# Loading w2 in blocks of six from ScalarE's DMA queue, with a new cost model and new priorities for the order of all instructions

## The chip, the cores and the metric

The kernel runs on one core of one Trainium2 chip. The metric is the device time of one execution in microseconds (us). A single core has no second die to compare with, so all runs count as fast ones, but executions of one program still differ: most by under 0.5%, a few by 1%. Medians over several executions are given with their range.

## The reference, cut to what matters

Two layers, each made of sliding-window attention and an MLP, on 2048 tokens of width 576:

```python
# x: [1, 2048, 576]; 32 heads of 18, window 256; MLP width F = 4608; bf16 inputs
x = x + A(layernorm(x))       # qkv = x @ wqkv; masked softmax(q k^T * 18**-0.5) v; @ wo
x = x + B(layernorm(x))       # gelu(x @ w1 + b1) @ w2 + b2
x = x + A(layernorm(x))       # the same weights again
x = x + B(layernorm(x))
```

## The kernel before

The 2048 tokens are worked off in groups of 512, four per layer. Its buffers hold four ninths of w1 and half of w2, so both are loaded anew for each group. Every operation is described once as a task (engine, buffers read and written, an estimated cost, a priority). A scheduler written in Python plays the tasks through on estimated costs and fixes one order of instructions for each engine. `nudge` shifts the priority of whole stages: `q1.0` is a part of the projections of group 1, `t0` the tail of group 0 (output projection, residual, layernorm), `ma0` the first MLP matmuls, and so on.

```python
PL.nudge = {"ld0+": 36.49, "eb0": 11.82, "q1.0": -3.43, ...}        # cut

def w1_load(prio, reads=()):                                        # cut
    dma("sp", w1_sb[:, sl, 0:2048]..., B_w1[0:512, cols]..., cls="w1", cost=0.55, ...)
    for b in range(2):                                              # the last 64 rows
        dma("sp", w1_sb[64 * b:64 * b + 64, sl, 2048:2304]..., cls="w1", cost=0.6, ...)

def w2_load(hf, prio, gate=False):
    for pr in range(NFH // 2):                                      # nine pairs a half
        f0 = hf * NFH + 2 * pr
        dma("sp", w2_sb[:, 2 * pr:2 * pr + 2, :], B_w2[f0 * P:(f0 + 2) * P, :]...,
            writes=[f"w2s{pr}"], cls="w2", ring=9, cost=0.55, lat=2.0, move=0.88, desc=256, prio=prio)

def tail(k, prio):                                                  # cut
    for i in range(nt):                                             # attention output, transposed by DMA
        add("sp", lambda e, i=i: e.dma_start_transpose(attT[:, :, i * 128:(i + 1) * 128], attq[:, i, :]), ...)
    for i in range(nt):
        bs = two_out(lambda c, i=i: attT[...], lambda c, s: wo_sb[...], ...)   # output projection on TensorE

# ln_norm_T, cut: the normalise on VectorE, then a DMA transpose from SyncE
add("dve", lambda e: e.tensor_scalar(xn[:, sl, 0:D], s[:, t, :], mv_all[:, t, 0:1], rstd[:, t:t + 1], ...), cost=0.6, ...)
add("sp", lambda e: e.dma_start_transpose(dst[:, :, i * 128:(i + 1) * 128], xn[:, sl, :]), ...)

def x_load(a, cnt, reads, prio):                                    # the residual, from GpSimd
    dma("pool", x_res[:, a:a + cnt, :], x_dram[...]..., cls="xr", ...)
```

Each DMA is issued by one engine (`"sp"` is SyncE, `"act"` ScalarE, `"pool"` GpSimd), and each engine takes its instructions in the order that the scheduler fixed. Nearly all weights and all transposes go through SyncE.

The softmax here doesn't subtract the row's maximum and nothing guards it: scores larger than these inputs give would overflow.

## Time and profile before

| | before |
|---|---|
| time, median of 3 | 945.84 us (945.45 to 946.3) |
| TensorE busy | 910.2 us of a span of 940.9 us |
| ScalarE busy | 593.4 us |
| bytes in SyncE's queue (q1) | 120.96 MB of 130.10 MB |

TensorE is at work for 97% of the span. What can be won is its idle time and what its records hide, so the waits of TensorE are the view to read, and the other engines matter where they end such a wait. The profiled execution of the kernel before took 942.78 us, some 3 us less than its median. In line numbers, L524 before and L530 after is the helper that issues every plain DMA, so loads are told apart by their tiles and sizes. Three terms recur: a transfer is *issued* while its engine hands it to the DMA engines, and it *lands* when all its data have arrived; the *granted clock* (PEclk) is the share of its full clock that TensorE was given, in these records either 1.00 or, for some us at a time, 0.50 ("half clock").

### The profile page before, as it was taken

Reading aid. Unit: us, or ns where it says so; the run is one execution under the profiler, and the core shown is the slowest. Engines: PE = TensorE matmul, PEld = TensorE weight load, DVE = VectorE, ACT = ScalarE, POOL = GpSimd, SP = SyncE. Lnnn points to the kernel's source line nnn. Section 1 sums busy time; section 2 is a strip of 40 time slices with the busy share of each in tenths; the row PEclk is TensorE's granted clock in tenths of the full one; section 3 lists DMA queues with packets and bytes.
Section 4 is the critical chain, followed back from the end, with each engine's and each line's share of the span. In section 5 each row is a group of like instructions: output and inputs, shape, how many; then the busy total and the mean of one; then the engine's idle time right before and its main releaser. Section 6 shows DMA issues by size and latency. Waiting matters only on the chain. (4 is left out here: it accounts for less than half of the span.)

```text
span 940.9 us, 22724 instructions
## 1 busy us (share of the span) xinstructions
PE 910.2 (97%) x9394; PEld 559.5 (59%) x9394; DVE 319.3 (34%) x796; ACT 593.4 (63%) x717; POOL 372.1 (40%) x507
## 2 busy tenths in 40 slices
PE   9888998999999999989999999999999999999998
PEld 6555474664755747455674666656566574656556
DVE  6647132641217511154420832135132330241001
ACT  3787675576756658656465567756776587852541
POOL 3877352353514425144250644515443163720100
PEclk9999999999999999999999999999999999999999
DMA  9995729725196160965439434594526916094440
GB/s 225 153 219 113 212 60 247 191 56 169 21 218 163 16 204 13 249 130 140 133 45 270 79 93 123 99 252 77 158 71 121 252 52 203 13 233 140 151 140 26
DMA packets 232470, 130.10 MB, mean 138 GB/s; under 512 B 142384, under 2 KB 230192, under 8 KB 232368
## 3 DMA queue, kind: packets, MB, share of 16 engines
q1 hardware_dynamic: 223056, 120.96, 53.8%
q0 software_dynamic: 6880, 5.03, 3.7%
q10 hardware_dynamic: 2432, 2.65, 0.9%
q8 instruction: 75, 1.23, 0.5%
q14 instruction: 27, 0.22, 0.1%
HBM read 91.87 MB, written 2.36 MB: 100 GB/s over the span
## 5 line engine op out<-in xcount | busy, mean ns | idle before, releaser
L744 ACT ACTIVATE pT<-ps 128x1024 bf16<-128x1024 f32 (+2 forms) x384 | 348.3, 970 | 138.7 <-PE ps L735 137.6
L765 POOL TENSOR_SCALAR_AFFINE_SELECT pT<-pT 128x512 bf16<-128x512 bf16 (+1 forms) x368 | 281.8, 789 | 288.9 <-ACT pT L744 258.8
L903 PE MATMUL ps<-w_sb,hT 128*128 128x288 bf16 x2304 | 318.0, 287 | 3.1 <-DVE x_res L816 1.8
L878 ACT ACTIVATE hT<-ps,b1col 128x512 bf16<-128x512 f32 x288 | 197.0, 688 | 176.1 <-PE ps L875 175.9
L875 PE MATMUL ps<-xnTm,w_sb 128*128 128x512 bf16 x1152 | 263.8, 380 | 0.0
L903 PEld LDWEIGHTS ps<-w_sb,hT 128*128 128x128 bf16 x2304 | 212.0, 98 | 74.8 <-issue 15.1
L875 PEld LDWEIGHTS ps<-xnTm,w_sb 128*128 128x128 bf16 x1152 | 106.2, 98 | 142.0 <-issue 26.6
L816 DVE TENSOR_TENSOR x_res<-ps,x_res 128x288 f32<-128x288 f32 x160 | 71.2, 449 | 312.0 <-PE ps L903 242.9
L665 PE MATMUL ps<-wqkv,xnTa 128*128 128x288 bf16 x960 | 136.9, 288 | 6.3 <-DVE qn L700 4.1
L665 PEld LDWEIGHTS ps<-wqkv,xnTa 128*128 128x128 bf16 x960 | 86.4, 98 | 42.5 <-DVE qn L700 8.6
L782 PEld LDWEIGHTS ps<-vA,pT 128*128 128x128 bf16 x2880 | 94.8, 96 | 25.3 <-issue 9.7
L782 PE MATMUL ps<-vA,pT 128*128 128x20 bf16 x2880 | 100.4, 171 | 3.5 <-POOL pT L765 2.7
L700 DVE CAST qn<-ps 128x288 bf16<-128x288 f32 x120 | 54.3, 455 | 106.1 <-PE ps L665 103.5
L885 POOL TENSOR_TENSOR x_res<-x_res,b2bc 128x576 f32<-128x576 f32 x32 | 44.9, 1402 | 97.1 <-ACT hT L878 97.1
L735 PE MATMUL ps<-qT,kT 32*128 32x384 bf16 (+2 forms) x1216 | 64.4, 277 | 3.4 <-DMA kT<-qn 1.2
L591 POOL TENSOR_SCALAR vtmp<-mv_all 128x1 f32<-128x1 f32 (+1 forms) x43 | 8.8, 205 | 116.9 <-DVE mv_all L582 115.7
L665 PE MATMUL ps<-wo_sb,attT 128*128 128x288 bf16 x320 | 45.5, 289 | 6.7 <-DMA attT<-attq 5.8
L580 DVE BATCH_NORM_STATS2 st_all<-x_res 128x6 f32<-128x288 f32 x104 | 44.8, 447 | 7.5 <-DMA x_res<-in_A_x_dram 6.3
L863 PE MATMUL ps<-xnTm,w_sb 64*128 64x512 bf16 x288 | 45.3, 384 | 1.0 <-ACT pT L744 0.7
L603 DVE TENSOR_SCALAR xn<-x_res,mv_all,rstd 128x576 bf16<-128x576 f32 x52 | 38.9, 754 | 15.2 <-DMA xnTm<-xn 5.8
L665 PEld LDWEIGHTS ps<-wo_sb,attT 128*128 128x128 bf16 x320 | 29.6, 98 | 19.9 <-DMA attT<-attq 6.7
L819 DVE TENSOR_TENSOR xn<-ps,x_res 128x288 bf16<-128x288 f32 x32 | 14.4, 454 | 77.2 <-PE ps L903 75.6
(39 smaller groups left out, 270.3 us busy)
## 6 DMA issues: line engine op xcount, KB each, us to landing
w_sb<-in_B_w_dram SPq DMA_DIRECT2D x144, 288.0 KB, 4.5
w_sb<-in_B_w_dram SPq DMA_DIRECT2D x72, 512.0 KB, 4.5
w_sb<-in_B_w_dram SPq DMA_DIRECT2D x144, 32.0 KB, 4.1
x_res<-in_A_x_dram POOLq DMA_DIRECT2D x4, 1152.0 KB, 7.8
out_dram<-xn SPq DMA_DIRECT2D x16, 144.0 KB, 1.8
wqkv<-in_A_wqkv_dram ACTq DMA_DIRECT2D x3, 576.0 KB, 7.2
hT<-in_A_x_dram SPq DMA_DIRECT2D x2, 576.0 KB, 4.4
wo_sb<-in_A_wo_dram ACTq DMA_DIRECT2D x1, 576.0 KB, 6.6
```

The lines of the kernel that those rows point to most:

```text
L665: ins = e.matmul(bank(bs[o])[:, 0:HB], lhs(c), rhs(c, o * HB), start=(c == 0), stop=(c == KD - 1))
L700: add("dve", lambda e, b=bs[o], dst=dst: e.tensor_copy(dst, bank(b)[:, 0:HB].rearrange("p (h d) -> p h d", d=DH)), reads=[bs[o]], writes=[ ...
L735: ins = e.matmul(two(bs[j // 2])[:, j % 2, col:col + nq * 128], k_of(T0 + so)[0][32 * j:32 * j + 32, g, :], qs[32 * j:32 * j + 32, g, qo * ...
L744: add("act", lambda e, h2=h2: e.activation(pT[:, sl, 2 * h2:2 * h2 + 2, lo:hi], two(bs[h2])[:, :, lo:hi], ACT.Exp, scale=SCALE), reads=[bs ...
L765: add("pool", lambda e, ap=ap, pat=pat, sgn=sgn, kind=kind: e.affine_select(ap, ap, pattern=pat, compare_op=(ALU.is_ge if kind == "d" else ...
L782: ins = e.matmul(bank(B_O)[:, o:o + VW], pT[:, sl, j, col + qi * 128:col + (qi + 1) * 128], vA[:, (T0 + so) % VS, 4 * g + j, :], start=(fi ...
L816: add("dve", lambda e: e.tensor_tensor(x_res[:, t, sl], bank(b)[:, 0:HB], x_res[:, t, sl], ALU.add), reads=[b], writes=[f"x{t}h{hh}"], cos ...
L863: ins = e.matmul(bank(bk)[:, 0:n], w1_sb[64 * b:64 * b + 64, sl, col:col + 128], xnTm[64 * b:64 * b + 64, k % 2, 4, 0:n], start=True, stop ...
L875: ins = e.matmul(bank(bk)[:, 0:n], w1_sb[:, sl, col:col + 128], xnTm[:, k % 2, c, 0:n], start=False, stop=(c == 3))
L878: add("act", lambda e, ff=ff, fl=fl, bk=bk: e.activation(hT[:, fl, 0:n], bank(bk)[:, 0:n], ACT.Gelu_apprx_tanh, bias=b1col[:, ff:ff + 1]), ...
L885: add("pool", lambda e, t=t: e.tensor_tensor(x_res[:, t, :], x_res[:, t, :], b2bc[:, :], ALU.add), reads=["b2", f"h{fs[0]}"], writes=X(t), ...
L903: ins = e.matmul(bank(b)[:, 0:HB], hT[:, fl, i * 128:(i + 1) * 128], w2_sb[:, fl, hh * HB:(hh + 1) * HB], start=(fl == 0), stop=(fl == NFH ...
```

## The change

It has three parts. w2 is loaded in blocks of six slices (864 KB) by ScalarE's DMA queue, instead of pairs (288 KB) by SyncE's. The scheduler's model now has a queue for each issuing engine that shares the DMA engines, and operation costs taken from traces. The priorities were found anew by annealing on that model, so every engine's order changes.

```diff
+    WB = 6
-    PL.nudge = {"ld0+": 36.49, "eb0": 11.82, "q1.0": -3.43, ...}
+    PL.nudge = {"le0+": 6.85, "q1.0": -1.09, "q1.1": -1.98, ...}          # all values new; cut
     def w2_load(hf, prio, gate=False):
-        for pr in range(NFH // 2):
-            f0 = hf * NFH + 2 * pr
-            dma("sp", w2_sb[:, 2 * pr:2 * pr + 2, :], ..., writes=[f"w2s{pr}"], cls="w2", ring=9, cost=0.55, ..., desc=256)
+        for b in range(NFH // WB):
+            f0 = hf * NFH + WB * b
+            dma("act", w2_sb[:, WB * b:WB * b + WB, :], ..., writes=[f"w2s{b}"], cls="w2", ring=NFH // WB, cost=0.55, ..., desc=128 * WB)
     # scheduler: one modelled queue for each issuing engine
-                done = max(dma_free, st + t.cost + t.lat) + t.move
+                at = max(served.get(t.eng, 0.0), st + t.cost + min(t.lat, 2.0))
+                done = at + t.move
+                for o in served:
+                    if o != t.eng and served[o] > at:
+                        both = min(t.move, served[o] - at)
+                        served[o] += both
+                        done += both                                     # cut
     # costs, some of about twenty
-            reads=res + [f"mv{t}", f"rstd{t}"], writes=[f"xn{sl}"], cost=0.6, prio=prio)
+            reads=res + [f"mv{t}", f"rstd{t}"], writes=[f"xn{sl}"], cost=0.67 if src is None else 0.45, lat=0.14, prio=prio)
-            reads=[f"vt{t}" for t in ts] + ["nhalf"], writes=rds, cost=0.4, prio=prio)
+            reads=[f"vt{t}" for t in ts] + ["nhalf"], writes=rds, cost=0.4 + 0.155 * n, lat=0.08, prio=prio)
```

## The prediction

> **What bounds the kernel now.** I read the page's busy table first, then the busy time per stretch, the waits of PE, the waits of the DMA queue on SyncE, and last the timeline around the longest waits. The busy table and the slices say TensorE:
>
> ```profile
> PE 910.2 (97%) x9394; PEld 559.5 (59%) x9394; DVE 319.3 (34%) x796; ACT 593.4 (63%) x717; POOL 372.1 (40%) x507
> ...
> PE   9888998999999999989999999999999999999998
> ...
> DMA  9995729725196160965439434594526916094440
> ```
>
> PE stands still for only 940.9 - 910.2 = 30.7 us by these records, and DMA engines, ScalarE and GpSimd all have room. So no change that leaves the matmuls alone can gain more than those 30.7 us plus waits that the records hide. They do hide some: the record of a 128x288 matmul is 287 ns (groups table), yet by their start times such matmuls follow each other every 122 ns, so a wait of 150 ns between two of them does not show as idle.
>
> I therefore also added up the start-to-start distances of all matmuls. At the usual spacing of each kind (122 ns for 288 columns, 216 ns for 512, 25 ns for the 20-column ones) all matmuls but the scores make about 807 us. The score groups and the changes from one kind of matmul to another, at what such a change usually takes here (96 to 260 ns), make about 100 us more. What lies above the usual value is 33 us: 13 us before 94 us, 3.9 us in 141 to 188, 4.5 us in 376 to 423, and mostly 0 to 2 us in other stretches of 47 us. Those 33 us are the whole prize for a better order and better timed transfers, with a few us of ramp, warm-up matmuls and tail beside them.
>
> The stretches show where it stands still (PE busy is the second number, then PEld, DVE, ACT and POOL; near the end PEclk and the DMA share):
>
> ```profile
> 20.00:40.00 20.00, 16.14 (x191) 9.27 (x189) 13.60 (x43) 13.23 (x19) 13.82 (x19) 0.91 1.63 138
> 60.00:80.00 20.00, 17.06 (x277) 11.11 (x277) 9.47 (x25) 17.31 (x21) 14.00 (x20) 1.00 0.80 156
> 160.00:180.00 20.00, 18.04 (x112) 9.99 (x113) 13.26 (x39) 7.17 (x10) 3.41 (x8) 0.91 0.94 247
> 400.00:420.00 20.00, 16.29 (x208) 11.73 (x207) 10.12 (x26) 11.62 (x15) 7.90 (x13) 1.00 0.67 137
> 580.00:600.00 20.00, 20.00 (x303) 14.35 (x300) 4.11 (x10) 16.07 (x18) 12.42 (x17) 1.00 0.01 2
> ```
>
> The ramp (the first 100 us, where w2 plays no part) loses most: 100 - 88.6 = 11.4 us idle. Then two spots stand out. In both, the waits of PE name one cause, the DMA transpose of the attention output:
>
> ```profile
> PE ps L665 <- DMA attT<-attq: 5.8, 2, 3.1
> PE ps L665 <- DVE qn L700: 4.1, 9, 0.9
> PE ps L782 <- POOL pT L765: 2.7, 8, 0.6
> PE ps L735 <- DMA kT<-qn: 2.1, 2, 1.2
> ```
>
> The timeline of the first spot shows SyncE's queue issuing one transpose, then six weight loads in 7.44 us, then the next transpose, while PE waits 3.08 us:
>
> ```profile
> 153.19 1.23 SPq L826 DMA_TRANSPOSE attT<-attq  x1
> ...
> 154.52 7.44 SPq L524 DMA_DIRECT2D w_sb<-in_B_w_dram  x6
> ...
> 161.96 2.00 PE L665 MATMUL ps<-wo_sb,attT 128*128 128x288 bf16 x10 [3.08 <-DMA attT<-attq]
> 162.01 1.29 SPq L826 DMA_TRANSPOSE attT<-attq  x1
> ```
>
> And the queue's own waits show that loads which wait for a buffer hold up everything behind them:
>
> ```profile
> SPq L524 <- PE ps L903: 89.5, 17, 25.8
> ```
>
> These are w2 loads waiting for the second MLP matmuls to free their buffer, up to 25.8 us at a time. Most of it costs nothing, as nothing urgent stood behind.
>
> **What the Trainium skill says.** "DMA: Bandwidth & Descriptors", section "Issuing engines are not separate DMA queues": transfers started from different engines run on the same 16 DMA engines, and a second issuer only saves issue time. The same page, section "Queues, rings and completion order": each DMA engine takes turns between the queues that have work, a packet at a time. So no bandwidth is gained, but a transpose need not stand behind a burst of w2 in the same queue. Before, nearly all goes through one queue (q1, 120.96 MB of 130.10 MB), so the trace can't show it yet. "Trace Analysis", section "Per-instruction lifecycle": the record of such an issue covers descriptor generation, not the movement. The trace agrees: a weight load issues in 0.515 us at the median and lands after 4.5 us. "TensorE: Matmul & The Clock Gate", section "Why this matters for your kernels": idle gaps of about 3 us drop the clock. The trace agrees in part: PEclk is 0.91 in 160 to 180, after the 3.08 us gap, and also in 20 to 40, but stays 1.00 after the 2.68 us gap near 410.
>
> **The change, part by part.**
> *Removed from SyncE:* 144 w2 loads of 288 KB at 0.515 us = 74 us of issuing, more where the ring was full (the longest took 2.834 us). The queue's issuing now is 360 x about 0.55 us for weights (197 us summed from the trace) plus 156 transposes (214 us), so it falls from some 411 us to some 330 us, and the buffer waits leave it as well. Off PE's path except at the two attT spots. There I expect most of the 5.8 us back, some 4.5 us, and the half clock from 173.1 to 176.5 us in the trace, worth 3.4 / 2 = 1.7 us: **-6 us**.
> *Added to ScalarE:* 16 half loads x 3 blocks = 48 issues of 864 KB. Before, ACT issued six loads in 3.76 us, 0.63 us each: 48 x 0.63 = 30 us. The diff's own bookkeeping counts 768 descriptors a block against 2048, so the third block of a half should wait for space, which I guess at 1.5 us: 16 x 1.5 = 24 us more. ScalarE stands still 940.9 - 593.4 = 347 us, so 54 us fit, but it runs in order: an issue ahead of an exp or a gelu delays it. In the busiest mixed stretches (17.3 of 20 us) this can reach PE. I allow **+2 us**.
> *Bytes:* the same, 2.65 MB per half. A block of six is what one matmul task reads anyway, so waiting for six in place of three pairs costs nothing.
> *Moved:* every order on every engine, from new costs and nudges. The new costs agree better with the profile where I can compare: a residual add 0.375 + 0.14 = 0.515 us against a record of 0.449; a normalise 0.67 + 0.14 against 0.754; the small 64-column normalise 0.38 + 0.14 against 0.468, formerly 0.12; rstd for four now 1.02 against about 1.03 in the timeline, formerly 0.4. An order made with such costs should leave fewer of the short waits (qn, affine select, rstd). Of the 33 us above the usual, 6 are counted already; of the other 27 I take a third: **-9 us**. This is a guess, since the ramp's dependencies are real and the old order had been tuned too.
> Sum: -6 + 2 - 9 = -13 us, and I add -1 us for fewer warm-up matmuls filling gaps (62 now, 35 of them before any data is there). 945.84 - 14 = about **932 us**.
>
> **The rivals.**
> *ScalarE becomes the hindrance:* its queue now waits for the second MLP matmuls to free w2, as SyncE did for 89.5 us, and every exp and gelu behind waits too. For it: ScalarE is strictly in order and feeds PE twice, through exp and gelu. Against it: the new order puts issues where the model sees the buffer free, and the engine has 37% room. It would take back 5 to 15 us: 937 to 947.
> *The transfers were hidden anyway:* attT alone is 5.8 us, and most long queue waits have nothing urgent behind them. Then the order alone decides and the gain is under 6 us: 940 to 946.
> *The order is the main thing:* if the corrected model removes most of the 33 us, including the ramp, it saves 20 to 25 us: 921 to 926. Against it: the waits over the usual are near zero already in half of the stretches, and 13 us sit in a ramp whose first steps depend on each other.
>
> **Range and chances.** My sum gives 932; 33 us of prize, none of it needing new resources, makes slower unlikely. A 2% gain needs 926.9 us, thus 19 us, more than half of the prize: 0.27. Within 2%: 0.70. Slower by 2% would need ScalarE to stall for 19 us on PE's path: 0.03. Eight times in ten: 920 to 944.
>
> **What would show it.** Right: PE busy time nearly the same or a little less, idle down from 30.7 to under 20 us; no wait on attT over 1 us; queue waits on w2 gone from SyncE; a second hardware queue with 42 MB (48 x 864 KB); PEclk 1.00 in the stretches after 100 us; 48 issues on ScalarE of 0.6 us at the median with some over 2 us. The step on ScalarE is wrong if its waits on PE within w2 issues add up to over 10 us with PE idle beside them. The step on the order is wrong if idle outside the attT spots stays at some 25 us. The prediction as a whole fails if hardware lets w2 bursts slow the transposes by sharing the engines, so that kT, qT or attT land later than now (3.7 to 4.0 us) and PE waits there in new places, or if the new order cuts the number of changes between kinds of matmul, which I left as it is.

## The result, and the profile after

| | before | after |
|---|---|---|
| median, same rounds | 945.68 us (945.45 to 946.3, 4 runs) | 937.97 us (937.35 to 938.3, 4 runs) |
| ratio | | 0.9917, 95% interval 0.99 to 0.9934: the same within 2% |
| span of the profiled execution | 940.9 us | 936.2 us |

Ratios are the mean time of one kernel's fast runs over that of the other's fast runs of the same rounds, so not quite the ratio of the medians. The gain is 7.7 us where 14 were predicted.

The page of the kernel after, its busy table, TensorE's slices and the two hardware queues (packets, MB, share of the engines' time):

```profile
PE 903.7 (97%) x9336; PEld 562.5 (60%) x9382; DVE 316.5 (34%) x796; ACT 593.9 (63%) x717; POOL 370.5 (40%) x507
...
PE   8798999999999999999999999999999999999998
...
q1 hardware_dynamic: 183888, 78.48, 40.0%
q10 hardware_dynamic: 40064, 45.13, 15.4%
```

The second queue now carries w2, 48 x 864 KB = 42.5 MB more than its former 2.65 MB. The weight loads (PEld) count 12 fewer, which are warm-up matmuls. Matmul records: 9336 against 9382 weight loads, so 46 are missing, and the busy sums of the two traces cannot be subtracted to a few us.

The stretches that the prediction showed, and three more (40 to 60, 820 to 840 of both kernels). Columns: stretch, length, then busy us of PE, PEld, DVE, ACT and POOL with counts, granted clock, DMA share, GB/s. After:

```profile
20.00:40.00 20.00, 16.29 (x198) 10.79 (x199) 14.01 (x42) 11.14 (x16) 12.06 (x16) 0.94 1.78 145
40.00:60.00 20.00, 16.01 (x208) 9.94 (x206) 11.71 (x22) 12.82 (x18) 12.04 (x17) 0.81 1.11 213
60.00:80.00 20.00, 17.59 (x298) 11.11 (x290) 8.44 (x21) 18.91 (x25) 15.12 (x21) 1.00 0.81 148
160.00:180.00 20.00, 19.78 (x133) 10.53 (x132) 8.24 (x25) 11.65 (x16) 2.95 (x6) 1.00 1.16 295
400.00:420.00 20.00, 19.34 (x228) 14.14 (x227) 18.97 (x49) 10.52 (x14) 10.74 (x18) 1.00 0.56 117
...
820.00:840.00 20.00, 18.00 (x109) 9.01 (x108) 10.76 (x30) 9.07 (x14) 2.96 (x8) 1.00 0.86 189
```

And before, for the two stretches that the prediction did not show:

```profile
40.00:60.00 20.00, 18.44 (x286) 11.88 (x285) 10.13 (x24) 16.26 (x23) 15.35 (x22) 1.00 1.24 249
820.00:840.00 20.00, 20.00 (x180) 11.02 (x178) 7.31 (x21) 12.35 (x17) 6.10 (x10) 1.00 0.89 229
```

Both bad spots are mended: TensorE is busy 19.78 us in 160 to 180 where it was 18.04, and 19.34 in 400 to 420 where it was 16.29. But two stretches got worse. In 40 to 60 it fell from 18.44 to 16.01 us of 20, at a mean clock of 0.81 instead of 1.00, and in 820 to 840 from 20.00 to 18.00.

TensorE's waits after (total us, times, longest):

```profile
PE ps L742 <- ACT pT L751: 5.5, 15, 1.1
PE ps L672 <- DVE qn L707: 4.5, 6, 2.0
PE ps L789 <- DVE attq L804: 2.6, 3, 1.4
PE ps L672 <- DMA attT<-attq: 2.1, 2, 1.9
PE ps L672 <- DVE vA L694: 2.0, 4, 1.1
```

The wait on attT fell from 5.8 to 2.1 us. The largest wait is now the one on ScalarE's exponentials, 5.5 us against 1.6 before.

To see where the time went I subtracted from the time, for both traces, the usual cost of every matmul issued so far (by its kind, from the spacing of weight loads). The difference of the two curves, after minus before, is +3.5 us at 160, +0.4 at 180, -2.0 at 400, -5.1 at 420, -7.5 at 800, -4.3 at 860 and -4.8 at 920. (A second working of the same sum gave +3.5, +0.6, -2.0, -5.0, -6.8, -4.9 and -4.8, so single stretches are good to some 0.7 us.) So the ramp lost 3.5 us; the two attT spots gained 3.1 us each; all else between 180 and 800 gained 4.8 us; the stretch of 800 to 860 gave 3.2 us back, and after it some 0.5 us came in again. The sum is the difference of the two spans, 4.7 us; the other 3 us of the median are the lucky execution that was profiled of the kernel before.

The curve leaves out the changes from one kind of matmul to another, and the new order has fewer of them: 762 in place of 788, or 751 in place of 765 without the warm-up matmuls. At the median spacing of each kind of change in the two traces that is about 3 us less, an estimate; no run isolates it.

### The profile page after: what moved, and what is told of

The parts are those of the page before. It is cut to its first block, busy times and chain, and to the rows that moved or that the text cites. A ratio compares the mean times of both kernels' runs of the same rounds, so it can differ in the third digit from the quotient of the medians.

```text
span 936.2 us, 22505 instructions
## 1 busy us (share of the span) xinstructions
PE 903.7 (97%) x9336; PEld 562.5 (60%) x9382; DVE 316.5 (34%) x796; ACT 593.9 (63%) x717; POOL 370.5 (40%) x507
## 4 chain that ended last, share of the span: by engine, by line
PE 82%; DMA 5%; DVE 4%; issue 3%; ACT 2%; POOL 2%; SPq 1%; POOLq 0%; DVEq 0%
PE ps L910 28%; PE ps L882 24%; PE ps L672 13%; PE ps L789 7%; PE ps L742 5%; PE ps L870 4%; DMA attT<-attq 2%; ACT pT L751 2%; DMA hT<-in_A_x_dram 1%; DMA qT<-qn 1%; DVE xn L609 1%; POOL pT L772 1%; PE ps L573 1%; SPq L714 1%; POOL x_res L892 0%
## 5 line engine op out<-in xcount | busy, mean ns | idle before, releaser
L910 PE MATMUL ps<-w_sb,hT 128*128 128x288 bf16 x2304 | 314.0, 286 | 0.4 <-DVE x_res L823 0.4
L882 PE MATMUL ps<-xnTm,w_sb 128*128 128x512 bf16 x1106 | 258.9, 379 | 4.0 <-issue 1.9
L799 DVE RECIPROCAL rinv<-ps 128x16 f32<-128x16 f32 x64 | 16.4, 256 | 72.4 <-PE ps L789 72.4
L742 PEld LDWEIGHTS ps<-qT,kT 32*128 32x128 bf16 x1216 | 19.6, 92 | 33.5 <-issue 22.0
```

The lines of the kernel that those rows point to most:

```text
L742: ins = e.matmul(two(bs[j // 2])[:, j % 2, col:col + nq * 128], k_of(T0 + so)[0][32 * j:32 * j + 32, g, :], qs[32 * j:32 * j + 32, g, qo * ...
L882: ins = e.matmul(bank(bk)[:, 0:n], w1_sb[:, sl, col:col + 128], xnTm[:, k % 2, c, 0:n], start=False, stop=(c == 3))
L910: ins = e.matmul(bank(b)[:, 0:HB], hT[:, fl, i * 128:(i + 1) * 128], w2_sb[:, fl, hh * HB:(hh + 1) * HB], start=(fl == 0), stop=(fl == NFH ...
```

## The experiments

Twelve kernels ran, in three sets of four, each set on another chip with its own runs of the kernel before (medians 946.24, 945.02 and 946.39 us). Medians of different sets are compared only roughly; the ratio to the kernel before of the same set is the safer number.

| kernel | set | median us (range) | ratio to before, 95% interval |
|---|---|---|---|
| x0, the kernel after again | 1 | 937.79 (936.3 to 948.39) | 0.9927 (0.9884 to 0.997) |
| x1, after, w2 sixes from SyncE | 1 | 942.87 (939.43 to 944.91) | 0.9957 (0.9924 to 0.999) |
| x3, before, w2 sixes from ScalarE | 1 | 951.7 (948.93 to 955.17) | 1.0058 (1.0027 to 1.009) |
| x4, after, one GpSimd load later | 1 | 936.43 (934.03 to 939.79) | 0.9897 (0.9867 to 0.9928) |
| x2, before, w2 pairs from ScalarE | 2 | 952.16 (947.87 to 955.78) | 1.0064 (1.0035 to 1.0094) |
| x5, after, no nudges | 2 | 953.28 (953.21 to 954.09) | 1.0084 (1.0059 to 1.0108) |
| x6, before, no nudges | 2 | 952.26 (949.2 to 958.38) | 1.0079 (1.0042 to 1.0116) |
| x7, before, x load later | 2 | 941.23 (940.26 to 944.33) | 0.9955 (0.9932 to 0.9978) |
| x8, after, ramp mended | 3 | 935.72 (934.74 to 936.31) | 0.9883 (0.9861 to 0.9905) |
| x9, after, w2 pairs from ScalarE | 3 | 947.59 (947.32 to 949.73) | 1.0014 (0.9995 to 1.0033) |
| x10, x8 and the x load later | 3 | 936.85 (935.32 to 938.22) | 0.9895 (0.9875 to 0.9916) |
| x11, x4 and the x load later | 3 | 937.14 (935.67 to 938.51) | 0.9898 (0.9879 to 0.9918) |

Most edits are made where the finished order is turned into instructions (`S.add`), after the scheduler has run. So an edit moves what it names and leaves the order of everything else as it was.

### The control

> The changed kernel once more, unedited, as the control of this set. Both theories: 938 us, ratio to the kernel before 0.9917 as measured, that is 0.990 to 0.994. Anything outside that says how much the chip itself moves the time.

Five of its six executions lie within 936.3 to 940.2 us. The profiled one took 948.39. Same program, same order, and yet in 390 to 395 us the DMA engines moved 100 GB/s, where the first trace of this kernel shows 331. First the slow execution, then the first trace of the same kernel:

```profile
390.00:395.00 5.00, 5.00 (x28) 2.29 (x27) 0.46 (x1) 2.75 (x4) 0.00 (x0) 1.00 1.22 100
```

```profile
390.00:395.00 5.00, 4.95 (x28) 2.17 (x29) 0.46 (x1) 2.76 (x5) 0.00 (x0) 1.00 1.15 331
```

The DMA share is the same 1.2, so the engines were as occupied, with a third of the result. One transpose then took 4.14 us to issue (1.3 us is usual) and TensorE waited 4.20 us on attT from 403.5 on. I have no run that shows why, and take from it only that one trace of an execution may mislead by 1%.

### The queue alone, in the old order: x3 and x2

The edit keeps the order of the kernel before, but w2 goes out of ScalarE's queue, in sixes (x3) or in its old pairs (x2):

```diff
-                self.S.add(t.eng, t.fn, names(t.reads), names(t.writes), dma=t.dma, ring=t.ring)
+                # x2: the same loads, another engine
+                self.S.add("act" if t.dma == "w2" else t.eng, t.fn, names(t.reads), names(t.writes), dma=t.dma, ring=t.ring)
+                # x3: three pairs kept back, then one load of six slices from "act" in the place of the third
```

> The kernel before with its order kept on every engine; only w2 goes to ScalarE's queue, three pair loads merged into one of six at the place of the third. Theory A: the two attT waits of 3.1 and 2.7 us shrink, 938 to 941 us. Theory B: no gain by itself, 944 to 947 us, or even slower, since ScalarE now waits at places that its order was not planned for.

> The kernel before with its order kept; the 144 w2 pair loads issued from ScalarE's queue, each at its planned place, none merged. The six-block version of the same was slower than the kernel before by 0.6%. If the larger block made that loss (a block waits for its last pair, and comes as one burst): 943 to 947 us here. If the queue made it (ScalarE now waits for w2's buffers at places its order was not planned for, and w2 runs beside w1 instead of behind it): 949 to 953 us again.

Both are slower than before by 0.6%, and alike: 951.7 and 952.16 us. The waits on attT grew from 5.8 to 10.4 us (x3; 10.5 in x2), the opposite of what the prediction promised:

```profile
PE ps L665 <- DMA attT<-attq: 10.4, 4, 5.3
```

SyncE's queue in x3 at the spot that the prediction showed of before:

```profile
154.21 1.35 SPq L826 DMA_TRANSPOSE attT<-attq  x1
155.66 6.21 SPq L524 DMA_DIRECT2D w_sb<-in_B_w_dram  x3
161.92 1.68 SPq L826 DMA_TRANSPOSE attT<-attq  x1
```

Before, six loads stood between these two transposes for 7.44 us. By their destination shapes three were w2 (2.83, 1.60 and 0.91 us) and three w1 (0.73, 0.48 and 0.60 us). Without the w2 loads the same three w1 loads, 1.8 us before, take 6.21 us to issue, one of them 3.40 us. So the time there was hardly the issuing of w2 itself; it passes to whatever stands in the queue next.

And the loads between were not what TensorE waited for. It wanted the **first** transpose of the four, the one issued ahead of the six loads. The time from issue to landing of the four attT transposes at this spot, first before, then x3, then the kernel after:

```profile
DMA to landing us min/median/max: 3.2/4.3/8.7
```

```profile
DMA to landing us min/median/max: 5.6/7.3/11.0
```

```profile
DMA to landing us min/median/max: 8.6/9.4/10.1
```

The longest of before is the first transpose: issued at 153.19, it landed some 8.7 us later, just before TensorE went on at 161.96. In x3 the same one took 11.0 us (11.3 in x2), from 154.21 on, and TensorE went on at 165.26. The prediction had read the timeline wrongly: the six loads stood behind the transpose that TensorE wanted, so they did not delay its issue. It was slow to land while the DMA engines were busy throughout (share 1.3 from 152 to 158 us in both); x7 below supports this as the reason. A likely reason for the extra 2.3 us is that w2 loads that used to stand behind the transpose in one queue now take turns with it from a second one, as the Trainium skill, "DMA: Bandwidth & Descriptors", section "Queues, rings and completion order", has it. The landing times fit that, and so does x1 below: in one and the same order the median of these four is 6.0 us with w2 in SyncE's queue and 9.4 with w2 in ScalarE's.

The second spot is another case. Of the kernel before:

```profile
404.00 1.73 SPq L524 DMA_DIRECT2D w_sb<-in_B_w_dram  x3
...
405.84 6.01 SPq L826 DMA_TRANSPOSE attT<-attq  x4
...
410.11 0.79 PE L665 MATMUL ps<-wo_sb,attT 128*128 128x288 bf16 x5 [2.68 <-DMA attT<-attq]
```

VectorE had finished attq at 402.33, and the transpose did stand in the queue behind loads until 405.84. But by their shapes all three are w1, so moving w2 does not free it: in x2 the wait here is 2.67 us again, and in x3, where attq came later than the loads, 1.16. The waits on attT of x2 and x3 grew at the first spot (5.55 and 5.29 us, from 3.08) and came anew near 630 us (2.29 and 3.37); by the curve of lost time they lost in other stretches too.

### The queue and the block size undone, in the new order: x1 and x9

x1 is the kernel after with the same blocks of six issued from SyncE. x9 is the kernel after with each block split into three pairs that ScalarE issues one after another, 144 issues in place of 48.

```diff
+                self.S.add("sp" if t.dma == "w2" else t.eng, ...)                        # x1
+    for i in range(3):                                                                   # x9
+        S.add("act", PAIR[t.idx][i], names(t.reads), [f"{t.writes[0]}_{i}"], dma="w2", ring=9)
```

> The changed kernel with every instruction of TensorE, VectorE, ScalarE's compute and GpSimd in the same order; only the 48 w2 issues go from ScalarE's queue to SyncE's, at the place in the order that the plan gave them. Theory A (the queue is the gain: transposes no longer stand behind w2): the gain is lost, 943 to 950 us, and TensorE waits on attT again. Theory B (the new order is the gain and w2's queue hardly matters): 937 to 940 us.

> Edit of the kernel after: each w2 block of six (864 KB) is loaded by three transfers of 288 KB one after another from ScalarE's queue, so 144 issues in place of 48; every order is kept. Theory S (the size of a block does nothing for the time by itself, it only saves issues): 937 to 940 us, ScalarE's w2 issues 144 at about 0.37 us, thus 53 us in place of 18, and TensorE waits for ScalarE no more than 1 us longer in sum. Rival B (block size matters, for the issues delay exps and gelus): 941 us or more, with TensorE's waits on ScalarE's results up by over 2 us.

x1 is 5.1 us slower than the control by the medians (3 us by the ratios, with intervals that overlap; its six executions span 939.4 to 944.9, five of the control's six 936.3 to 940.2), between the ranges of the two theories. Its trace has a wait of 1.87 us for a w2 load at 514.7 us that the kernel after has not. It tells more by what did not change. It has no wait on attT at 160 or 400 us. The first output projection starts at 172.9 us in x1 and at 173.3 us in the kernel after, while its transposes are issued from 159.84 on in the latter: the new order puts some 13 us of other matmuls between. Before, TensorE reached the output projection at 158.9 us (161.96 less the wait of 3.08), 5.7 us after the first issue, and waited there. In the kernel after the transposes land later than before, 8.6 to 10.1 us after issue (2.7 to 9.4 in x1), and nobody waits for them. The output projection there, x1 first and then the kernel after:

```profile
L672 PE MATMUL ps<-wo_sb,attT x40: 283/286/296, 172.9 to 183.7; 128*128 128x288 bf16 x40
```

```profile
L672 PE MATMUL ps<-wo_sb,attT x40: 282/286/296, 173.3 to 184.1; 128*128 128x288 bf16 x40
```

**So it is the order that removed the attT waits at both spots, not the queue.** At the first spot this holds in all eight traces of kernels with the new order and its nudges. At the second it holds in six: in x0 and x4 a wait is back (4.20 and 2.99 us, until 407.7 and 401.2), with landings of up to 10.3 and 9.2 us where the first trace has 5.5. There the new order leaves less room than some executions need.

x9 is 947.59 us, some 10 us slower than the kernel after, and the theory that the block size does nothing by itself falls. The 144 issues took 76.0 us in sum (17 of them over 0.7 us, the longest 1.81 us), against 18.4 us for 48 (longest 0.56 us). One place in x9's timeline:

```profile
314.60 2.75 ACTq L659 DMA_DIRECT2D w_sb<-in_B_w_dram  x3
...
317.47 1.94 ACT L751 ACTIVATE pT<-ps 128x1024 bf16<-128x1024 f32 x2 [2.49 <-PE ps L910]
...
318.55 0.40 PE L742 MATMUL ps<-qT,kT 32*128 32x384 bf16 x8 [1.70 <-ACT pT L751]
```

Three issues hold ScalarE for 2.75 us, the next exponential starts right after them, and TensorE waits 1.70 us for it. (The view blames ScalarE's gap on TensorE's last result; that one had long been there.) In sum TensorE waits 13.9 us for results of ScalarE in x9 and 6.6 us in the kernel after: 7.3 of the 10 us. The six-slice block matters because it needs a third of the issues and these never met a full queue. In the old order, where w2 pairs were slow for another reason, the same difference did not show (x2 against x3).

### The priorities alone: x5 and x6

Each kernel without its nudges:

```diff
-    PL.nudge = {...}
+    PL.nudge = {}
```

> The changed kernel with an empty table of annealed priorities; new costs, new queue. If annealing is what makes either order good, it loses more than 10 us: 948 to 960 us. If the new costs alone make a good order: under 943 us.

> The kernel before with an empty table of annealed priorities. Together with the run above it compares old and new costs with queue without annealing. If the corrected costs are worth much by themselves, this one is over 8 us slower than the changed kernel without its table; if not, the two are within 4 us.

953.28 and 952.26 us, ratios of 1.0084 and 1.0079: without annealed priorities the new model, costs and queue gain nothing over the old. Annealing is worth 15 us in the kernel after (953.28 to 937.97) and 7 us in the kernel before. I can't say from these runs how much of the larger figure is owed to the better model as the ground to anneal on, and how much to a longer or luckier search.

### The ramp: x4 and x8

The kernel after in the ramp, VectorE, GpSimd and TensorE together:

```profile
41.59 0.83 POOL L530 DMA_DIRECT2D x_res<-in_A_x_dram  x1
41.66 2.63 DVE L609 TENSOR_SCALAR xn<-hT,mv_all,rstd 128x576 bf16<-128x576 bf16 x1
...
42.43 3.54 POOL L772 TENSOR_SCALAR_AFFINE_SELECT pT<-pT 128x1024 bf16<-128x1024 bf16 x5
...
44.22 0.44 DVE L707 CAST qn<-ps 128x288 bf16<-128x288 f32 x1
44.59 2.23 DVE L609 TENSOR_SCALAR xn<-hT,mv_all,rstd 128x576 bf16<-128x576 bf16 x3
...
44.72 1.38 PE L672 MATMUL ps<-wqkv,xnTa 128*128 128x288 bf16 x5 [1.96 <-DVE qn L707]
```

One normalise takes 2.63 us where others of its kind take 0.42 us undisturbed. It starts 0.07 us after GpSimd's issue of the x_res load and ends 0.18 us after the second of the affine selects behind it. The cast behind it is late, TensorE waits 1.96 us, and 1.1 us more for a cast of v behind the block of three. The granted clock is at half from 44.3 to 51.1 us (and from 37.5 to 40.9). The Trainium skill, "SBUF — State Buffer", section "Who interferes with whom", says that VectorE in certain fast modes, which this operation can enter, and GpSimd share a pair of ports, and that the second of them is blocked until the first is through. The 2.63 us agree; no run shows which mode the operation was in.

x4 lets GpSimd issue that load six places later. x8 does so as well, and puts the three normalises one by one between the casts of v and of the q and k normalises on VectorE, while TensorE, ScalarE and SyncE keep their order.

```diff
+    if t.dma == "xr" and ST["x0"] is None:          # x4 and x8: hold the first x_res load back
+        ST["x0"] = t
+        return
+    if norm and ST["norms"] < 3:                    # x8: hold normalises 2 to 4 back, ...
+        ST["held"].append(t)
+        return
+    if ST["held"] and t.eng == "dve" and t.stage.startswith("q1."):
+        put(ST["held"].pop(0))                      # ... one after each cast
```

> The changed kernel with one GpSimd instruction moved: the first issue of the fp32 load of x goes six places later in GpSimd's order, past the time of four bf16 normalisations on VectorE. In the trace of the changed kernel the first of these took 2.63 us beside that issue (0.43 us is usual), TensorE then stood still 1.96 and 1.14 us and ran at half clock in 48.1 to 51.5 and 54.9 to 61.8 us. Theory C (that collision is what the new order lost in the ramp): the normalisation falls under 1.2 us, and the time to 932 to 936 us. Rival D (the normalisation is held by the affine selects anyway, or the clock dips come from the idle in general): no change, 937 to 939 us.

(Two clock spans in this text are 10.6 us late: I read them on the recording's own clock. They are 37.5 to 40.9 and 44.3 to 51.1 us.)

> Edit of the kernel after: GpSimd's first x_res load is issued six places later (as in the run called x4), and the three bf16 normalises that stood one after another on VectorE in the ramp are put one at a time between the casts of v and the q/k normalises; TensorE, ScalarE and SyncE keep their order. Theory R (the 3.5 us that the new order loses in the ramp come from the block of normalises on VectorE and the half clock that follows): the 1.2 us waits of TensorE on qn and vA near 45 us are under 0.6 us each, no half-clock window between 40 and 60 us, 934 to 936 us, ratio to the kernel before 0.987 to 0.990. Rival T (the transposes of the normalised tiles now come later and TensorE waits for them instead): new waits on xn of over 1 us before 70 us, 937 to 939 us.

In x4 the normalise takes 1.19 us, now beside one affine select:

```profile
40.19 1.19 DVE L609 TENSOR_SCALAR xn<-hT,mv_all,rstd 128x576 bf16<-128x576 bf16 x1 [0.91 <-POOL rstd L599]
```

Its median is 936.43 us, 1.4 below the control and 0.4 above the range of theory C; the intervals of the ratios overlap. In x8 the median is 935.72 us. Two stretches, x8 first and then the kernel after:

```profile
44.00:48.00 4.00, 3.47 (x62) 2.53 (x63) 3.11 (x8) 2.22 (x3) 0.95 (x3) 1.00 0.56 107
48.00:52.00 4.00, 2.96 (x47) 1.70 (x46) 1.45 (x4) 2.49 (x5) 2.89 (x4) 1.00 0.84 211
```

```profile
44.00:48.00 4.00, 2.14 (x9) 1.08 (x10) 3.18 (x6) 0.33 (x1) 1.97 (x4) 0.54 1.76 322
48.00:52.00 4.00, 3.96 (x59) 2.58 (x58) 1.63 (x4) 2.26 (x3) 0.36 (x1) 0.61 0.37 77
```

In x8 the clock stays full in the whole run up to the end, and by the curve of lost time x8 is 3.1 us ahead of the kernel after at 120 us, nearly the 3.5 us that the new order had lost in the ramp. The waits on vA are 0.6 us at most, as expected; one of 1.1 us on qn stays, which the theory had at under 0.6.

The times alone do not settle the ramp, but the traces of all eight kernels with this order do. In the four with the load beside the normalise (the kernel after, x0, x1, x9) it takes 2.63 to 3.81 us, the half clock after it lasts some 6.8 us, and by the curve they are 2.1 to 4.9 us behind before at 120 us. In the four with the load later (x4, x8, x10, x11) it takes 1.19 to 1.20 us, the half clock lasts 3.4 us in three and is absent in x8, and they are between 0.1 us ahead and 0.8 us behind. So the collision and what it sets off is shown as the cause of the ramp's loss. That the single normalises of x8 add anything to x4 is not: 0.9883 and 0.9897 have overlapping intervals, and x10, with the same ramp as x8, has a half clock from 44.0 to 47.5 us. By the median x8 is the fastest kernel.

### The load in the attention burst: x7, x10 and x11

In the kernel before, GpSimd loads 1152 KB of the residual (tiles 8 to 11) just ahead of the late transposes. x7 moves this load behind the tail of group 1, counted from 0; x10 and x11 do so in x8 and x4.

```diff
+    if STATE["left"] and t.dma == "xr" and "x8h0" in t.writes:
+        HELD.append(t)                              # put again when the tail of the group is through
+        return
```

> The kernel before with one GpSimd instruction moved: the second layer-one load of x (1152 KB written as fp32, not needed before some 250 us) goes behind the attention tail of the second chunk, where DMA ran at 306 GB/s and TensorE waited 3.08 us for attT. Theory E (that wait is a burst of all transfers together, x loads among them, and not w2 ahead in the same queue): the wait falls under 1.5 us, the half clock behind it goes, 941 to 944 us. Theory A (the queue's order makes it): the wait stays near 3 us and the time at 945 to 946 us.

> Edit of the kernel after: the ramp's edits of x8_ramp, and GpSimd's x load for tiles 8 to 11 moved behind the tail of the first token group (as in x7 for the kernel before, where it gained 0.45%). Theory L (the load in the middle of the attention burst delays other transfers in the new order too): 931 to 934 us, at least 2 us under x8_ramp. Rival N (in the new order TensorE does not wait in 140 to 185 us, so that moving the load is worth nothing): within 1 us of x8_ramp.

> Edit of the kernel after: only GpSimd's loads are moved, the first x_res load six places later (as in x4) and the load for tiles 8 to 11 behind the tail of the first token group; no compute order changes. Theory L: 933 to 935 us, at least 2 us under the 936.4 us of x4. Rival N: 935.5 to 937.5 us, as x4. If x8_ramp equals this one or is slower, the normalise order of x8 is worth nothing.

In the old order it gains 0.45% (941.23 us). In its profile the attT wait at this spot falls from 3.1 to 2.2 us, not below the 1.5 I had written, the first transpose lands after 7.9 us in place of 8.7, and the half clock there is gone (two others stand at 194 and 406 us). So the sum of all transfers in that stretch, not the queue of one of them, was part of the old wait. In the new order no gain is seen: x10 is 1.1 us above x8, and x11 is 0.7 us above x4. That fits a TensorE that no longer waits in that stretch.

## Why the prediction was right or wrong

The time, 937.97 us, lies in the range of 920 to 944 and within 2%. The sum behind 932 was wrong in its terms, and its errors partly offset one another, which is luck.

- **"I expect most of the 5.8 us back ... -6 us".** The size held, by luck: the two spots gave 3.1 us each by the curve of lost time, and the half clock there is gone. The reason failed. The prediction saw six loads between two transposes and concluded that taking the w2 loads out of the queue would free the transpose. But at the first spot TensorE waited for the transpose ahead of those loads, which took 8.7 us to land, and at the second the loads ahead of it were w1. Taking w2 to the other queue made the 8.7 us 11.0, the waits longer (10.4 us in sum) and the kernel 0.6% slower. The order removed the waits, at the first spot by giving TensorE some 13 us between issue and use in place of 5.7. A new wait on attT of 1.9 us at 827 us took part of it back, against the prediction's own sign of no such wait over 1 us. The prediction's own warning, that w2 would share the engines and let the transposes land later, came true: 5.2 us at the median for attT against 4.0 over the whole run.
- **"The half clock from 173.1 to 176.5 us".** These two times are a mistake of mine: they are on the recording's clock, 10.5 us later than the span's. It is 162.6 to 166.0 us, just after the wait, so the argument stands.
- **"54 us fit ... I allow +2 us".** The 48 issues cost 0.374 us each at the median, 18.4 us in sum, not 30, and none met a full queue, against 24 us guessed. TensorE's waits for ScalarE rose from 3.0 to 6.6 us, but they are 6.7 us in x1, where SyncE issues w2: they come from the order. The term for the queue is zero. The rival in which ScalarE becomes the hindrance is real only for pairs (x9).
- **"A block of six ... costs nothing".** Right, but too timid: the block of six is worth some 10 us against pairs in this order, for the number of issues.
- **"Of the other 27 I take a third: -9 us".** This is the step that failed. Outside the attT spots the trace shows 4.8 us gained between 180 and 800, 3.5 us lost in the ramp and 2.7 us lost after 800: +1.4 us, or about -1.5 us when the 3 us of the lucky profiled execution are allowed for. The prize was also summed too high: 3584 x 122, 1440 x 216 and 2880 x 25 ns make 820 us, not 807, which leaves some 20 us above the usual in place of 33. And the changes between kinds of matmul, which the prediction left as they were, are worth about 3 us by the estimate above. Good costs did not make a good ramp, because a cost is not a property of an operation alone: the normalise, modelled at 0.45 + 0.14 us, took 2.63 us beside GpSimd, and a half clock followed, which a model of fixed costs cannot see. x8 wins 3 us of it back. Of the costs that the prediction compared, one does not agree better: the residual add's old 0.46 us is nearer to the record of 0.449 than the new 0.515.
- **"-1 us for fewer warm-up matmuls".** Twelve fewer were issued. No run isolates them.
- **What would show it.** The second queue has its 42.5 MB, and the queue's waits for w2's buffers are gone from SyncE. Its issuing fell from 411 to 353 us, not to 330, since the transposes now take 230 us to issue (214 before). PEclk is 1.00 in the stretches after 100 us, as said; the loss sits before, with 0.81 in 40 to 60. The idle time of under 20 us is not reached: some 32 us by the records (the 46 missing ones make up some 2 of them, by an estimate of 0.05 us for the gap that each leaves).

The 2 x 2 of set 1 tells the rest, in medians: old order, old queue 946.2; old order, new queue 951.7; new order, old queue 942.9; new order, new queue 937.8. The queue costs 5.5 us in one order, clear of noise, and gains 5.1 in the other, or 3 by the ratios, whose intervals overlap. No sum of parts, each valued alone, could have given 7.7.

## What to carry to other kernels

A finely tuned order fits the queues it was tuned with, so test a change of queue only together with an order made for it, and never add up what the parts are worth alone. Before blaming what stands between two transfers in a queue, look up which transfer the engine waited for and how long it took from issue to landing: here the DMA engines were busy throughout, another queue freed nothing, and an order that asked for the result later did. Look for operations that take several times their usual duration beside another engine, since here one such stall in a thin stretch went with a half-clock period twice as long as without it.

## What the Trainium skill lacked or had wrong

- "DMA: Bandwidth & Descriptors", section "Issuing engines are not separate DMA queues", says that a second issuer only saves issue time. These runs show a cost beside that saving: the same w2 loads moved to a second queue made the old order 5.5 us slower; a transpose in the first queue then landed after 11.0 us in place of 8.7, and three w1 loads there went from 1.8 to 6.2 us of issuing.
- "SBUF — State Buffer", section "Who interferes with whom", has the exclusive lock and examples of slowdowns, but not how long a DMA issue of GpSimd with the work behind it can hold up VectorE: here one normalise took 2.63 us in place of 0.42 (3.81 in three other traces), and 1.19 us when GpSimd's load was issued later.
- "DMA: Bandwidth & Descriptors" has a count of cycles for a copy's issue, but no page that I read gives the issue time of a load against its size or behind others: from ScalarE 864 KB took 0.374 us at the median and at most 0.56, while 288 KB took 0.37 us at the least, 0.48 at the median and up to 1.81 when issued three in a row.
- No page that I read says how far executions of one program can lie apart: 936.3 to 948.4 us here, with DMA at 331 and at 100 GB/s in the same 5 us.
